# Key factors and bounds of batch 0 shared by all batches, and the value matmuls dealt 5, 5, 4, 4 to the slots

## Chip, cores and metric

One core of one Trainium2 chip runs the whole kernel. The metric is device time in microseconds of one launch; lower is better.

## What is computed

Four batches of 12288 queries attend to 768 pooled keys each; keys and values are the same tensor. The attention's output goes, token by token, through a feed-forward layer of 1024 hidden units with a softmax gate and a normalization.

```python
def _attn_ref(q, kv, w_sr):
    kv_pool = kv.reshape(B, H // r, r, W // r, r, C).mean(axis=(2, 4))   # r = 4
    k = v = kv_pool.reshape(B, -1, C) @ w_sr                             # 768 keys, C = 128
    s = 1 / sqrt(C) * (q @ k.transpose(0, 2, 1))
    a = np.exp(s - s.max(-1, keepdims=True))
    a /= a.sum(-1, keepdims=True) + 1e-09
    return a @ v

def _moe_ref(x, w_in, w_out, g_ln):
    h = x @ w_in                                                         # 128 -> 1024
    e = np.exp(h - h.max(-1))
    solu = h * e / (e.sum(-1) + 1e-09)
    ln = (solu - mean(solu)) / sqrt(var(solu) + 1e-06) * g_ln
    return ln @ w_out                                                    # 1024 -> 128
```

## The kernel before

A tile is 128 tokens; there are 384 tiles, 96 to a batch, and 4 tiles make a group. The order of all work is written out by hand: the loop `for slot in range(NT)` issues, in each of 384 slots, one piece of every stage, each for another tile. Every engine runs its own queue in that order.

In slot S, TensorE (PE) does the scores `s` of tile S+1 (six matmuls of 384 columns, line 518), some of the 18 value matmuls `xa` of a group (512 columns, line 583), the hidden layer `h` of tile S-9 (six of 512 columns, line 636) and the output `o` of tile S-13 (24 of 128 columns, line 764). VectorE (DVE) does the row maximum `nm` of the scores of tile S (line 538), `u` of tile S-11 (line 674), `junkd`, the row maximum of `h`, of tile S-10 (line 644), and the low half of `phl` of tile S (line 549). In the first slot of a group's cycle it also does `xl`, `rz` and `ob`. ScalarE (ACT) does the exponentials `s` and `e`, the high half of `phl`, and `junk`. GpSimd (POOL) splits `u` into a high and a low 16-bit half `uhl` (lines 691 and 698) and adds up the keys of the next batch (`ka`, line 235). SyncE (SP) issues all DMAs of the loop: the transposes `pT` of `phl` and `uT` of `uhl`, and the loads of `q`, of `kv` and the stores of the output.

`s` and `h` share three PSUM buffers. So `s` of tile S+1 waits for `u` of tile S-11 to have read its `h`, and `h` of tile S-9 waits for `phl` of tile S to have read its `s`.

The 18 value matmuls of a group are dealt to four slots by `values` as 4, 5, 5, 4. In each slot but the first, one of them is issued ahead of `s` and the rest behind it. These four slots, called first to fourth below, are those with S mod 4 = 1, 2, 3, 0. A slot that has a matmul of the next batch's keys in it and is a first slot (`with_keys`) deals 3, 5, 5, 5, and its three go behind `o`.

The scores of batch 0 run on 32-bit halves of the keys (`kwh`, `kwl`). Those of batches 1 to 3 run on 16-bit halves `kh`, `kl` of keys scaled by a power of two that follows from the largest key norm of the batch. For each of batches 1 to 3, `key_steps` places the making of the keys at slots 69 to 92 of the batch before: the projection (`kv_k_pe`), squares (`kv_sq`), the norms by a matmul with ones and two maxima on DVE (`kv_norm_pe`, `kv_norm_max`), a scale per channel for the values (`kv_scale_v`), bounds and factors (`kv_bound`, `kv_factors`), `kh` on ACT, `kl` on DVE, and, for batches 1 and 2, the values by matmul with a diagonal (`kv_v_pe`). For batch 3 the values are turned by one DMA transpose (`kv_v_turn`). The loads of the next batch's `kv` and their additions run from slot -30 to slot 65 of a batch, so that one load or another is under way until about slot 253.

After the loop, `in_range` tests that every softmax sum in `z_all` is at least 0.5; where one isn't, the branch `general` computes everything again in a slower way.

Of the kernel before, what the change touches and what calls it, by code (L numbers as in the profile page):

```python
# [58 lines left out]
Z_LEAST = 0.5  # L59

# [4 lines left out]
def kernel(  # L65
# [179 lines left out]
    def kv_k_out(b, half):  # L245
        nc.scalar.copy(half_of("kT", b, half), state.pop(("pk", half))[:, :384])
# [14 lines left out]
    def kv_kh(b, half):  # L261
        nc.scalar.mul(half_of("kh", b, half), half_of("kT", b, half), state["kq", b][:, 0:1])

    def kv_kl(b, half):
        nc.vector.scalar_tensor_tensor(
            half_of("kl", b, half),
            half_of("kT", b, half),
            state["kq", b][:, 0:1],
            half_of("kh", b, half),
            op0=ALU.mult,  # L270
            op1=ALU.subtract,
        )

    def kv_factors(b, half):

        kq = state["kq", b]
        nc.vector.tensor_copy(kq[:, 0:1], state["knm", b][:, 2:3])
        nc.vector.reciprocal(kq[:, 1:2], kq[:, 0:1])
        nc.vector.tensor_scalar(kq[:, 1:2], kq[:, 1:2], SCALE, None, op0=ALU.mult)
# [40 lines left out]
    def kv_bound0(part):  # L320
        knm, bb, sv = state["knm", 0], state["bb", 0], state["sv", 0]
        if part == 0:
            nc.vector.tensor_reduce(knm[:, 2:3], knm[:, 0:2], axis=AX.X, op=ALU.max)
# [29 lines left out]
    def kv_bound(b, part):  # L353
# [13 lines left out]
        elif part == 1:  # L367
# [6 lines left out]
            kv_factors(b, 0)  # L374
# [6 lines left out]
    def kv_diag(b, half):  # L381
        state["dg", b] = bat.tile([P, P], F32, tag="dg", name=f"dg_{b}", bufs=1)
# [35 lines left out]
    def kv_v_scale(b, half):  # L418
# [3 lines left out]
            state["sv", b][:, 0:1],  # L422
# [140 lines left out]
    def values(g, qtr, part):  # L563
        share = {0: [0, 9, 9, 0], 1: [0, 6, 6, 6]}.get(g, [4, 5, 5, 4])
# [6 lines left out]
        cut = s0 + (s0 > 0)  # L571
# [229 lines left out]
    z_all = const.tile([P, NT], F32, name="z_all")  # L801
# [143 lines left out]
    def w_low():  # L945
        nc.gpsimd.tensor_tensor(wcl, gw, wch, op=ALU.subtract)

    fill_front = {1: [partial(kv_norm_max, 0, 0)]}
    fill = {
        0: [partial(kv_norm_pe, 0, 0), partial(kv_scale_v0, 0), w_scale],  # L950
        1: [
            partial(kv_norm_pe, 0, 1), partial(q_split, 1), partial(kv_scale_v0, 1),
            partial(kv_scale_v0, 2), partial(kv_diag, 0, 0), partial(q_low, 1), w_in_low,
        ],
        2: [partial(kv_norm_max, 0, 1), partial(kv_v_pe, 0, 0)],
# [10 lines left out]
        11: [w_low],  # L966
    }
# [44 lines left out]
    FRONT = (kv_scale_v, kv_bound)  # L1012
# [7 lines left out]
    for slot in range(NT):  # L1020
# [53 lines left out]
        for st in pairs:
            for f in st[1:]:
                if f.func is kv_norm_max:
                    f()
# [12 lines left out]
        for st in todo:  # L1090
# [3 lines left out]
            elif len(st) == 1 and st[0].func not in FRONT:  # L1094
# [185 lines left out]
```

## Time and profile before

| | us |
|---|---|
| median of 3 runs | 1868.81 |
| lowest and highest run | 1863.45, 1869.68 |
| the profiled execution's own time | 1865.23 |
| its span, first to last instruction | 1863.4 |
| busy: PE, DVE, ACT, POOL | 1829.8, 1794.2, 1747.4, 1662.0 |

The sums below are made against the profiled execution. A busy share is a mean over stretches; where the loop's steps start, and what an engine waited for just before, is read from the timeline of each engine. All times there are counted from the start of the span. The granted clock of TensorE is 0.999 of full speed over the span.

### The profile page before, as it was taken

What the parts mean: (1) busy time and instruction counts of PE and PEld (TensorE: products, weight loads), DVE (VectorE), ACT (ScalarE), POOL (GpSimd) and SP (SyncE); (2) the same over time, 40 slices, a digit from 0 to 9 for tenths busy, and PEclk for the clock granted to TensorE, in tenths of its full rate; (3) what the DMA queues carried; (4) which work ended last, traced back from release to release, by engine and by line L of the source; (5) the groups of instructions that cost most, each with busy time, mean ns of one, the idle gap of its engine ahead of it and who ended that gap; (6) DMA issues with size and microseconds to landing.
All of it is one profiled execution on the core that took longest, in us unless ns stands there. A gap on an engine that the chain in (4) does not pass through costs nothing.

```text
span 1863.4 us, 42816 instructions
## 1 busy us (share of the span) xinstructions
PE 1829.8 (98%) x15729; PEld 1185.2 (64%) x15729; DVE 1794.2 (96%) x2703; ACT 1747.4 (94%) x3124; POOL 1662.0 (89%) x1466
## 2 busy tenths in 40 slices
PE   8999999999999999999999999999999999999998
PEld 5667777766666656666666666666566666666666
DVE  7999999999999999999999999999999999999997
ACT  5999999999999999999999999999899999999997
POOL 5899999889999999989999999998888888888887
PEclk9999999999999999999999999999999999999999
DMA  8999999999999999999999999999999999999998
GB/s 301 209 225 240 243 240 239 241 225 222 240 232 240 247 227 241 238 239 238 216 242 234 241 240 243 237 237 223 207 227 226 235 228 220 232 227 232 227 216 171
DMA packets 1476891, 432.80 MB, mean 232 GB/s; under 512 B 1404608, under 2 KB 1457984, under 8 KB 1476416
## 3 DMA queue, kind: packets, MB, share of 16 engines
q1 hardware_dynamic: 1476528, 429.97, 113.7%
q8 instruction: 126, 2.06, 0.5%
q14 instruction: 93, 0.76, 0.1%
q10 hardware_dynamic: 144, 0.00, 0.0%
HBM read 52.50 MB, written 25.17 MB: 42 GB/s over the span
## 4 chain that ended last, share of the span: by engine, by line
PE 72%; DVE 9%; POOL 6%; DMA 5%; issue 4%; ACT 3%; SPq 0%; POOLq 0%; DVEq 0%; ACTq 0%
PE o L764 21%; PE h L636 20%; PE s L518 16%; PE xa L583 15%; DMA uT<-uhl 4%; POOL uhl L698 3%; DVE junkd L644 2%; DVE phl L549 2%; DVE nm L538 2%; POOL uhl L691 2%; DVE u L674 1%; DMA kv<-in_kv_dram 1%; ACT e L660 1%; ACT junk L739 1%; ACT phl L541 1%
## 5 line engine op out<-in xcount | busy, mean ns | idle before, releaser
L698 POOL TENSOR_TENSOR uhl<-u,uhl 128x1024 f16<-128x1024 f32 x382 | 814.6, 2133 | 31.6
L764 PEld LDWEIGHTS <-uT 128*128 128x128 f16 x9072 | 536.9, 98 | 96.8 <-DMA uT<-uhl 11.1
L764 PE MATMUL o<-wch,uT 128*128 128x128 f16 x6048 | 568.2, 219 | 4.8 <-DMA uT<-uhl 4.6
L764 PE MATMUL o<-wcl,uT 128*128 128x128 f16 x3024 | 525.9, 219 | 0.0
L674 DVE SCALAR_TENSOR_TENSOR u<-h,rz,e 128x1024 f32<-128x1024 f32 x384 | 491.2, 1279 | 22.2 <-ACT e L660 15.4
L691 POOL TENSOR_SCALAR uhl<-u 128x1024 f16<-128x1024 f32 x379 | 396.7, 1047 | 107.0 <-DVE u L674 99.4
L644 DVE TENSOR_SCALAR_CACHE_REDUCE junkd<-h,rz 128x1024 bf16<-128x1024 f32 x384 | 491.0, 1279 | 1.0 <-PE h L636 0.7
L583 PE MATMUL xa<-pT,vhl 128*128 128x512 f16 x1728 | 478.7, 380 | 0.0
L660 ACT ACTIVATE e<-h,nm,rz 128x1024 f32<-128x1024 f32 x384 | 458.5, 1194 | 3.7 <-DVE junkd L644 3.0
L739 ACT ACTIVATE junk<-u,su 128x1024 bf16<-128x1024 f32 x384 | 437.4, 1139 | 0.1
L539 ACT ACTIVATE s<-s,nm 128x768 f32<-128x768 f32 x384 | 334.5, 871 | 55.0 <-DVE nm L538 53.8
L538 DVE TENSOR_REDUCE nm<-s 128x1 f32<-128x768 f32 x384 | 365.0, 951 | 20.2 <-PE s L518 16.8
L549 DVE SCALAR_TENSOR_TENSOR phl<-s,phl 128x768 f16<-128x768 f32 x384 | 366.0, 953 | 1.7 <-ACT phl L541 1.4
L541 ACT ACTIVATE phl<-s 128x768 f16<-128x768 f32 x384 | 311.5, 811 | 12.1
L636 PEld LDWEIGHTS <-xh 128*128 128x128 f16 x1536 | 138.3, 97 | 214.8 <-issue 35.6
L583 PEld LDWEIGHTS <-vhl 128*128 128x128 f16 x1728 | 162.0, 98 | 132.9 <-issue 12.8
L636 PE MATMUL h<-w_in_h,xh 128*128 128x512 f16 x768 | 228.9, 379 | 9.2 <-DVE rz L618 5.4
L636 PE MATMUL h<-w_in_h,xl 128*128 128x512 f16 x768 | 228.4, 379 | 0.0
L636 PE MATMUL h<-w_in_l,xh 128*128 128x512 f16 x768 | 228.3, 379 | 0.0
L518 PEld LDWEIGHTS <-qh 128*128 128x128 f16 x1152 | 109.2, 98 | 68.3 <-DVE u L674 4.8
L518 PE MATMUL s<-kh,qh 128*128 128x384 f16 x576 | 140.8, 326 | 3.6 <-DVE u L674 3.6
L518 PE MATMUL s<-kh,ql 128*128 128x384 f16 x576 | 140.7, 326 | 0.0
(161 smaller groups left out, 1813.7 us busy)
## 6 DMA issues: line engine op xcount, KB each, us to landing
kv<-in_kv_dram SPq DMA_DIRECT2D x64, 384.0 KB, 4.4
qf<-in_q_dram SPq DMA_DIRECT2D x96, 256.0 KB, 3.3
out_dram<-ob SPq DMA_DIRECT2D x96, 256.0 KB, 2.8
pT<-phl SPq DMA_TRANSPOSE x384, 3.9
uT<-uhl SPq DMA_TRANSPOSE x378, 4.3
raw_in<-in_moe_w_in_dram SPq DMA_DIRECT2D x1, 1024.0 KB, 5.6
raw_out<-in_moe_w_out_dram SPq DMA_DIRECT2D x1, 1024.0 KB, 10.0
room<-uhl SPq DMA_TRANSPOSE x5, 3.9
```

What stands on the lines that cost most here:

```text
L518: nc.tensor.matmul(s[:, half, :384], lh[:, ts], rh[:, half * 384 : (half + 1) * 384], start=n == 0, stop=n == 2,)
L538: nc.vector.tensor_reduce(nm, s, axis=AX.XY, op=ALU.max, negate=True)
L549: nc.vector.scalar_tensor_tensor(phl[:, 1], state.pop(("s", t)), SC, phl[:, 0], op0=ALU.mult, op1=ALU.subtract)
L583: nc.tensor.matmul(xa, v[:, c, :], pT[:, :, a * NKC + c, :], start=n == 0, stop=n == len(seq) - 1)
L636: nc.tensor.matmul(h[:, hs], lh[:, ts], rh[:, hs], start=n == 0, stop=n == 2)
L644: nc.vector.tensor_scalar(junk, state["h", t], state["rz", g][1][:, j : j + 1], None, op0=ALU.mult, op1=ALU.min, accum_out=nm,)
L660: nc.scalar.activation(e, state["h", t], AF.Exp, bias=nm, scale=state["rz", g][0][:, js], accum_out=state["z2", g][:, js],)
L674: nc.vector.scalar_tensor_tensor(u, state.pop(("h", t)), state["rz", g][2][:, j : j + 1], state.pop(("e", t)), op0=ALU.mult, op1=ALU.mult, ...
L691: nc.gpsimd.tensor_scalar(uhl[:, 0, :], u, 1.0, 1.0, op0=ALU.mult, op1=ALU.mult)
L698: low.tensor_tensor(uhl[:, 1, :], u, uhl[:, 0, :], op=ALU.subtract)
L739: nc.scalar.activation(junk, u, AF.Square, scale=-float(DFF), bias=su, accum_out=state["v3", g][:, j : j + 1],)
L764: nc.tensor.matmul(po[:, ts], uT[:, a * NFC + c, :], w[:, c, :], start=start, stop=stop)
```

## The change

Batches 1 to 3 no longer have factors and bounds of their own. `sv` (scales per channel), `bb` (bounds), `kq` (factors), `knm` and the diagonal `dg` are those of batch 0. In batch 0 the largest key norm is replaced by the sum of all squares over 1024, a matmul of two columns (`kv_total_pe`) and one sum of two (`kv_total`); the bounds take a factor 32 for it. The keys of later batches are scaled by batch 0's factor as they leave PSUM (`kv_k_out`), so `kh` is a plain copy and `kl` a subtraction, which moves from DVE to POOL. `kv_norm_pe`, `kv_norm_max`, `kv_scale_v`, `kv_bound` and `kv_diag` are gone from the loop for batches 1 to 3. A step at slot 302 (`kv_fit`) puts six values for each channel into new columns of `z_all`, so that the test at the end also covers whether batch 0's scales fit the channel sums of the others. The values of batches 1 and 2 are made at slot 81 in place of 85. Groups of batches 1 to 3 deal their value matmuls 5, 5, 4, 4, and the second slot has none ahead of `s`.

```diff
-            ("kss", 2, F32, 1),
-            ("knm", 3, F32, 1),
+            ("kss", 2, F32, 4),
             ("vf", NK, F32, 1),
-            ("sv", 2, F32, 2),
-            ("bb", 5, F32, 2),
-            ("kq", 2, F32, 2),
+        for n, w in (("knm", 3), ("sv", 2), ("bb", 5), ("kq", 3), ("dg", P)):
+            state[n, b] = (
+                state[n, 0]
+                if 0 < b < B
...
     def kv_k_out(b, half):
-        nc.scalar.copy(half_of("kT", b, half), state.pop(("pk", half))[:, :384])
+        pk = state.pop(("pk", half))[:, :384]
+        if b < B:
+            nc.scalar.mul(half_of("kT", b, half), pk, state["kq", b][:, 0:1])
...
     def kv_kh(b, half):
-        nc.scalar.mul(half_of("kh", b, half), half_of("kT", b, half), state["kq", b][:, 0:1])
+        nc.scalar.copy(half_of("kh", b, half), half_of("kT", b, half))
 
     def kv_kl(b, half):
-        nc.vector.scalar_tensor_tensor(
...
+        nc.gpsimd.tensor_tensor(
+            half_of("kl", b, half), half_of("kT", b, half), half_of("kh", b, half), op=ALU.subtract
+        )
...
+    def kv_rescale():
+        small(state["dg", 0], state["dg", 0], state["kq", 0][:, 2:3])
+        nc.gpsimd.tensor_tensor(
+            root, state["sv", 0][:, 0:1], state["kq", 0][:, 2:3], op=ALU.mult
+        )
+
+    def kv_fit():
+        low, high = z_all[:, NT : NT + B - 1], z_all[:, NT + B - 1 :]
+        for b in range(1, B):
+            nc.gpsimd.tensor_tensor(
+                fit[:, b - 1 : b], state["kss", b][:, 0:1], state["kss", b][:, 1:2], op=ALU.add
+            )
+        small(fit[:, : B - 1], fit[:, : B - 1], root, 1.0 / SC)
+        small(low, fit[:, : B - 1], root, FIT_LEAST / SC)
+        nc.gpsimd.tensor_scalar(
+            high, low, -1.0 / FIT_LEAST, FIT_MOST, op0=ALU.mult, op1=ALU.add
+        )
...
+    def kv_total_pe():
+        state["pn", 0] = kv_psum(0, "pn_0")
+        nc.tensor.matmul(
+            state["pn", 0][:, :2], onesm, state["kss", 0], start=True, stop=True
+        )
...
     def values(g, qtr, part):
-        share = {0: [0, 9, 9, 0], 1: [0, 6, 6, 6]}.get(g, [4, 5, 5, 4])
+        share = {0: [0, 9, 9, 0], 1: [0, 6, 6, 6]}.get(
+            g, [4, 5, 5, 4] if wide(g + 2) else [5, 5, 4, 4]
+        )
...
-        cut = s0 + (s0 > 0)
+        cut = s0 + (s0 > 0 and (qtr > 1 or wide(g + 2)))
...
             (69, 0, kv_k_pe, kv_k_out), (73, 1, kv_k_pe, kv_k_out),
-            (86, 0, kv_kh), (87, 1, kv_kh),
-            (87, 0, kv_kl), (88, 1, kv_kl),
             (72, 0, kv_sq), (75, 1, kv_sq),
-            (78, 0, kv_scale_v), (79, 1, kv_scale_v), (80, 2, kv_scale_v),
-            (77, 0, kv_norm_pe, kv_norm_max), (81, 1, kv_norm_pe, kv_norm_max),
-            (83, 0, kv_bound), (84, 1, kv_bound), (85, 2, kv_bound),
+            (77, 0, kv_kh), (79, 1, kv_kh),
+            (78, 0, kv_kl), (80, 1, kv_kl),
...
-                (81, 0, kv_diag),
-                (85, 0, kv_v_pe, kv_v_out), (87, 0, kv_v_high), (88, 0, kv_v_low),
+                (81, 0, kv_v_pe, kv_v_out), (83, 0, kv_v_high), (84, 0, kv_v_low),
                 (89, 1, kv_v_pe, kv_v_out), (91, 1, kv_v_high), (92, 1, kv_v_low),
```

Three places show how the order moves. On PE, in the second slot of a group of batch 2 (its values `xa`, the scores `s` of the next tile, `o` of an earlier one), before:

```order
L764 LDWEIGHTS uT_14684
L764 MATMUL o_14819<-wch,uT_14684 128x128
L583 LDWEIGHTS vhl_7656
L583 MATMUL xa_14801<-pT_14429,vhl_7656 128x512
L518 LDWEIGHTS qh_14547
L518 MATMUL s_14861<-kh_7654,qh_14547 128x384
```

and now:

```order
L798 MATMUL o_14748<-wcl,uT_14616 128x128
L798 LDWEIGHTS uT_14616
L798 MATMUL o_14748<-wch,uT_14616 128x128
L550 LDWEIGHTS qh_14480
L550 MATMUL s_14789<-kh_7617,qh_14480 128x384
```

The value matmul that stood between `o` and `s` is gone from there; five follow `s` in place of four, and the third slot has three behind `s` in place of four.

On DVE, at slots 179 to 181 (slots 83 to 85 of batch 1, where the bounds `bb` and factors of batch 2 were made between the four steps of each tile), before:

```order
L549 SCALAR_TENSOR_TENSOR phl_12774<-s_12694,phl_12774 128x768
L360 TENSOR_REDUCE knm_7649<-knm_7649 128x1
L361 TENSOR_SCALAR bb_7652<-knm_7649,wmax_99 128x1
L364 TENSOR_SCALAR knm_7649<-knm_7649 128x1
L538 TENSOR_REDUCE nm_12842<-s_12780 128x1
L674 SCALAR_TENSOR_TENSOR u_12847,su_12848<-h_12724,rz_12702,e_12796 128x1024
L644 TENSOR_SCALAR junkd_12869,nm_169_12868<-h_12804,rz_12702 128x1024
L549 SCALAR_TENSOR_TENSOR phl_12845<-s_12780,phl_12845 128x768
L368 TENSOR_SCALAR bb_7652<-bb_7652 128x1
```

and now:

```order
L581 SCALAR_TENSOR_TENSOR phl_12731<-s_12651,phl_12731 128x768
L570 TENSOR_REDUCE nm_12794<-s_12736 128x1
L708 SCALAR_TENSOR_TENSOR u_12799,su_12800<-h_12683,rz_12659,e_12752 128x1024
L678 TENSOR_SCALAR junkd_12821,nm_169_12820<-h_12761,rz_12659 128x1024
L581 SCALAR_TENSOR_TENSOR phl_12797<-s_12736,phl_12797 128x768
L570 TENSOR_REDUCE nm_12868<-s_12803 128x1
```

Nothing but the tiles' own steps is left; over the whole program DVE has 80 instructions fewer.

On POOL, at slots 173 to 175 (slots 77 to 79 of batch 1), before:

```order
L235 TENSOR_TENSOR ka_12312<-kv_0_11505,kv_1_12088 128x384
L95 TENSOR_SCALAR sv_7651<-sv_7651 128x1
L96 TENSOR_TENSOR sv_7651<-sv_7651,mhalf 128x1
L691 TENSOR_SCALAR uhl_12489<-u_12478 128x1024
L698 TENSOR_TENSOR uhl_12489<-u_12478,uhl_12489 128x1024
L505 TENSOR_TENSOR ql_12468<-qf_12015,qh_12467 128x512
L691 TENSOR_SCALAR uhl_12560<-u_12546 128x1024
```

and now:

```order
L240 TENSOR_TENSOR ka_12275<-kv_0_11468,kv_1_12051 128x384
L725 TENSOR_SCALAR uhl_12448<-u_12438 128x1024
L732 TENSOR_TENSOR uhl_12448<-u_12438,uhl_12448 128x1024
L537 TENSOR_TENSOR ql_12431<-qf_11978,qh_12430 128x512
L274 TENSOR_TENSOR kl_7618<-kT_7613,kh_7617 128x384
L725 TENSOR_SCALAR uhl_12519<-u_12505 128x1024
```

The scale's steps are gone and the first half of `kl` stands behind `ql`, ahead of the next tile's `uhl`. SP's queue holds the same DMAs in the same order; the one transpose of batch 3's values was there already.

## Rows read from the trace of the kernel before

**Rows 1.** The page, part 1: busy time, share of the span, instructions.

```profile
PE 1829.8 (98%) x15729; PEld 1185.2 (64%) x15729; DVE 1794.2 (96%) x2703; ACT 1747.4 (94%) x3124; POOL 1662.0 (89%) x1466
```

**Rows 2.** Timeline, DVE, slots 317 to 321: start, us, instruction [idle before <-releaser].

```profile
1507.55 0.96 DVE L538 TENSOR_REDUCE nm<-s 128x1 f32<-128x768 f32 x1
...
1513.95 1.27 DVE L674 SCALAR_TENSOR_TENSOR u<-h,rz,e 128x1024 f32<-128x1024 f32 x1
...
1522.67 1.28 DVE L674 SCALAR_TENSOR_TENSOR u<-h,rz,e 128x1024 f32<-128x1024 f32 x1 [0.18 <-ACT e L660]
...
1525.09 0.95 DVE L549 SCALAR_TENSOR_TENSOR phl<-s,phl 128x768 f16<-128x768 f32 x1
1526.09 0.96 DVE L538 TENSOR_REDUCE nm<-s 128x1 f32<-128x768 f32 x1
```

**Rows 3.** Timeline, PE, the same group, its first and second slot.

```profile
1512.04 0.59 PE L583 MATMUL xa<-pT,vhl 128*128 128x512 f16 x2
1512.59 0.59 PE L636 MATMUL h<-w_in_h,xh 128*128 128x512 f16 x2
...
1515.22 0.38 PE L583 MATMUL xa<-pT,vhl 128*128 128x512 f16 x1
1515.44 0.49 PE L518 MATMUL s<-kh,qh 128*128 128x384 f16 x2
```

**Rows 4.** Timeline, DVE: nm at slots 65, 69, 93, 165, 169, 181, 185, 189, 257, 261, 285, 381.

```profile
310.12 0.96 DVE L538 TENSOR_REDUCE nm<-s 128x1 f32<-128x768 f32 x1 [0.24 <-PE s L518]
328.85 0.96 DVE L538 TENSOR_REDUCE nm<-s 128x1 f32<-128x768 f32 x1 [0.24 <-PE s L518]
448.74 0.96 DVE L538 TENSOR_REDUCE nm<-s 128x1 f32<-128x768 f32 x1 [0.44 <-PE s L518]
784.92 0.96 DVE L538 TENSOR_REDUCE nm<-s 128x1 f32<-128x768 f32 x1
804.23 0.96 DVE L538 TENSOR_REDUCE nm<-s 128x1 f32<-128x768 f32 x1 [0.37 <-PE s L518]
863.11 0.95 DVE L538 TENSOR_REDUCE nm<-s 128x1 f32<-128x768 f32 x1
885.07 0.94 DVE L538 TENSOR_REDUCE nm<-s 128x1 f32<-128x768 f32 x1
904.14 0.96 DVE L538 TENSOR_REDUCE nm<-s 128x1 f32<-128x768 f32 x1 [0.37 <-PE s L518]
1221.78 0.96 DVE L538 TENSOR_REDUCE nm<-s 128x1 f32<-128x768 f32 x1
1240.32 0.96 DVE L538 TENSOR_REDUCE nm<-s 128x1 f32<-128x768 f32 x1
1359.23 0.96 DVE L538 TENSOR_REDUCE nm<-s 128x1 f32<-128x768 f32 x1
1804.20 0.96 DVE L538 TENSOR_REDUCE nm<-s 128x1 f32<-128x768 f32 x1
```

**Rows 5.** Groups by line and form: count | busy us, mean ns | idle before.

```profile
L265 DVE SCALAR_TENSOR_TENSOR kl<-kT,kq,kh 128x384 f16<-128x384 f32 x6 | 12.3, 2051 | 0.0
L411 POOL TENSOR_TENSOR vhl<-vf,vhl 128x384 f16<-128x384 f32 x6 | 5.8, 969 | 0.0
L299 DVE TENSOR_REDUCE knm<-pn 128x1 f32<-128x384 f32 x8 | 4.4, 547 | 0.0
```

**Rows 6.** Timeline, SP's queue of DMAs: in batch 1, then in batch 3.

```profile
652.52 3.80 SPq L713 DMA_TRANSPOSE uT<-uhl  x1
656.38 0.57 SPq L471 DMA_DIRECT2D qf<-in_q_dram  x1
...
1518.84 1.85 SPq L713 DMA_TRANSPOSE uT<-uhl  x1
1521.65 1.41 SPq L552 DMA_TRANSPOSE pT<-phl  x1
```

**Rows 7.** Waits: engine line waited for: us in total, times, longest us.

```profile
PEld L764 <- DMA uT<-uhl: 11.1, 14, 1.6
```

More of the change, by code (lines that the diff above doesn't have):

```diff
@@ L59 @@
 Z_LEAST = 0.5
+FIT_LEAST = 32.0
+FIT_MOST = 4.4
+FIT_AT = 302
 SOON = {0: (), 1: (11, 12), 2: (21, 27), 3: (33, 39), 4: (45, 47), 5: (51, 54)}
@@ L245, in kv_k_out @@
     def kv_k_out(b, half):
-        nc.scalar.copy(half_of("kT", b, half), state.pop(("pk", half))[:, :384])
+        pk = state.pop(("pk", half))[:, :384]
+        if b < B:
+            nc.scalar.mul(half_of("kT", b, half), pk, state["kq", b][:, 0:1])
+        else:
+            nc.scalar.copy(half_of("kT", b, half), pk)
     def kv_wide_h(b, half):
@@ L261, in kv_kh, with kv_factors @@
     def kv_kh(b, half):
-        nc.scalar.mul(half_of("kh", b, half), half_of("kT", b, half), state["kq", b][:, 0:1])
+        nc.scalar.copy(half_of("kh", b, half), half_of("kT", b, half))
     def kv_kl(b, half):
-        nc.vector.scalar_tensor_tensor(
[L266 to L271, printed above, removed]
-        )
[L274 to L279, printed above, removed]
+        nc.gpsimd.tensor_tensor(
+            half_of("kl", b, half), half_of("kT", b, half), half_of("kh", b, half), op=ALU.subtract
+        )
+    def kv_factors():
+        kq = state["kq", 0]
+        nc.vector.tensor_copy(kq[:, 0:1], state["knm", 0][:, 2:3])
+        nc.vector.reciprocal(kq[:, 2:3], kq[:, 0:1])
+        nc.vector.tensor_scalar(kq[:, 1:2], kq[:, 2:3], SCALE, None, op0=ALU.mult)
+    def kv_rescale():
[14 more added lines that the diff above has]
+        )
     def kv_sq(b, half):
@@ L286, in kv_sq, with kv_total @@
             accum_out=state["kss", b][:, half : half + 1],
+        )
[4 more added lines that the diff above has]
+        )
+    def kv_total():
+        nc.vector.tensor_reduce(
+            state["knm", 0][:, 2:3], state.pop(("pn", 0))[:, :2], axis=AX.X, op=ALU.add
         )
@@ L332, in kv_bound0 @@
         else:
-            small(bb[:, 1:2], bb[:, 0:1], SC * 1e-3 * 2.0**15)
-            small(bb[:, 0:1], bb[:, 0:1], SC)
+            small(bb[:, 1:2], bb[:, 0:1], SC / 32 * 1e-3 * 2.0**15)
+            small(bb[:, 0:1], bb[:, 0:1], SC / 32)
             small(bb[:, 2:3], bb[:, 1:2], 1e-9)
@@ L381, in kv_diag @@
     def kv_diag(b, half):
-        state["dg", b] = bat.tile([P, P], F32, tag="dg", name=f"dg_{b}", bufs=1)
         nc.gpsimd.tensor_scalar(
@@ L421, in kv_v_scale @@
             half_of("kT", b, half),
-            state["sv", b][:, 0:1],
+            root,
             1.0,
@@ L563, in values @@
     def values(g, qtr, part):
[L564 removed]
+        share = {0: [0, 9, 9, 0], 1: [0, 6, 6, 6]}.get(
+            g, [4, 5, 5, 4] if wide(g + 2) else [5, 5, 4, 4]
+        )
         if with_keys(g):
@@ L798, in final_out @@
         nc.sync.dma_start(rows.rearrange("(j p) c -> p j c", p=P), ob)
-    z_all = const.tile([P, NT], F32, name="z_all")
+    z_all = const.tile([P, NT + 2 * (B - 1)], F32, name="z_all")
+    fit = const.tile([P, B], F32, name="fit")
+    root = fit[:, B - 1 : B]
     ident = const.tile([P, P], F32, name="ident")
@@ L966 @@
         11: [w_low],
+        14: [kv_factors],
+        17: [kv_rescale],
+        FIT_AT: [kv_fit],
     }
@@ L1027 @@
         todo = plan.pop(slot, [])
-        for st in todo:
-            if len(st) == 1 and st[0].func in FRONT:
-                st[0]()
         at(slot, scores_exp)
-        for f in fill_front.get(slot, []):
-            f()
         if slot <= LH:
@@ L1069 @@
             for f in st[1:]:
-                if f.func is not kv_norm_max:
-                    f()
+                f()
         if slot >= LH:
             at(slot, scores_split)
[L1074 to L1077, printed above, removed]
         at_soon(slot - NORM, values_recip)
@@ L1093 @@
                     f()
-            elif len(st) == 1 and st[0].func not in FRONT:
+            elif len(st) == 1:
                 st[0]()
@@ L1106, in in_range @@
             state["inside"] = const.tile([P, 1], BF16, name="inside")
-            good = const.tile([P, NT], BF16, name="good")
+            good = const.tile([P, NT + 2 * (B - 1)], BF16, name="good")
             nc.vector.tensor_scalar(
```

11 lines of the change are left out of this document (4 added, 7 removed).

## The prediction

> **What bounds the kernel now.** I read the busy shares first [rows 1]: PE 98%, DVE 96%, ACT 94%. With engines so even, no share says what a change is worth, so the next view is the timeline of DVE, taken at one row that every tile has, `nm`, at the first slot of groups. Its starts cut the span into stretches [rows 4]. From slot 285 to 381 (batch 3, 24 groups) it takes 444.97 us, 18.54 a group. From slot 65 to 69 (batch 0, 32-bit scores) it takes 18.73. From slot 189 to 257 (batch 2 with loads of `kv` in flight, 17 groups) 317.64, 18.69 a group. And the six groups of slots 69 to 93 of batches 0, 1 and 2, in which the next batch's keys are made, take 119.89, 119.22 and 118.91 us, where 112.38 (six of 18.73), 111.24 and 111.24 would be the plain loop: 7.51, 7.98 and 7.67 too much, 23.2 us together. That is where the change works first.
>
> What holds the plain loop at 18.54 is seen on DVE and PE in one group. On DVE [rows 2] one `nm` of a first slot starts at 1507.55 and the next at 1526.09. Just before the latter `phl` began at 1525.09 and took 0.95. DVE instructions follow each other with an overlap of about 0.08, so `nm` could have started at 1525.96; it waited 0.13 for its scores. Before that `u` waited for `e` of ACT. Take the 0.13 away, and a chain of DVE and ACT alone is left: 18.41 a group. On PE [rows 3] value matmuls start 0.22 apart (1515.22, then 1515.44). The two of 1512.04 are through at 1512.48, but `h` starts at 1512.59, since `phl` has to read its buffer first: PE idles 0.11 in the first slot.
>
> **The keys leave DVE (forecast -16.3).** Per transition DVE loses two `kl` of 2.05 us, two maxima of 0.55 [rows 5], 5.2 us, and twenty-odd steps of one column. All of it stood between the steps of tiles on an engine that has next to no idle time, so it goes from the time as it stands. What stays is what PE does for the keys: projections at slots 69 and 73, values at 81 and 89 (batches 1 and 2 only). A group with such matmuls took 19.31 (slots 165 to 169) and 19.07 (slots 185 to 189, without any work on DVE for the keys) [rows 4]: 0.77 and 0.53 over 18.54. I take 0.6 for each; there are 4 + 4 + 2 = 10 of them, 6.0 us.
>
> ACT keeps its number of instructions; the scale moves from `kh` to `kT`. `kh` now stands at slots 77 and 79, the first hidden because ACT waits for `nm` in the second slot, the second in front of an `e` that DVE waits for. POOL gets two `kl`; its subtraction of the same shape takes 0.97 [rows 5]. POOL loses two steps for the scale, two for the bounds and the diagonal at the same slots, so its sum stays about level, but the values' split moves up to slots 83 and 84, in groups which are now 2 to 3.5 us shorter. `uhl` may come late, and behind it SP's transposes and `o`. I put 0.3 a transition for ACT and POOL together, 0.9; bounds 0 and 3. Sum: 23.2 - 6.0 - 0.9 = 16.3; bounds 23.2 - 5.3 = 17.9 and 23.2 - 7.7 - 3.0 = 12.5.
>
> One rule speaks against this part. `kl` on DVE takes 2.05 us, the norms' maximum over as many columns, out of PSUM, 0.55 [rows 5]: `kl` has both tensors in SBUF and seems to stand behind a POOL instruction. The Trainium skill, Perfetto Trace Analysis, section Optimizing Scalar/DVE Operations, says that GpSimd and DVE share an SBUF read port, so that moving work between the two might not help. By it the six `kl` would come back on DVE as waits, up to 5.8 us (six of 0.97), and the sum would be -10.5. The rows beside it speak against that: the four steps DVE does in these slots read at least one operand from PSUM, and none of them is longer next to the long POOL subtractions. So I leave it out.
>
> **The deal 5, 5, 4, 4 (forecast -5.6).** In the first slot a fifth value matmul fills the 0.11 for which PE waited, so `h` comes 0.11 later there. In the second slot nothing stands ahead of `s`, which gets 0.22 back: it starts 0.11 earlier, at 1515.33. It may not start before `u` of that slot is through, which starts on DVE at 1513.95 and takes 1.27 [rows 2], so it is through at 1515.22 and `s` hardly waits. `h` of the second slot then starts as now, behind `phl`. From there to the scores for which `nm` waited at 1526.09, PE has one value matmul less: they come 0.22 earlier. DVE waited 0.13 for them, so 0.13 is the gain, and the chain of DVE and ACT sets the end. Lower bound 0 (another wait takes its place).
>
> The groups that start at slots 97 to 377 have the new deal, 71, less six that deal 3, 5, 5, 5: 65. For the 29 from slot 257 on: 29 x 0.13 = 3.8 us. For the other 36, with loads of `kv` in flight, I do not trust it. There SP's queue issues without a break (`uT` at 652.52 for 3.80 us, the next DMA at 656.38), where in batch 3 it waits for its data (done at 1520.69, next at 1521.65) [rows 6], and PE waited 11.1 us in 14 places for `uT` [rows 7]. These groups took 18.69 though their own chain needs 18.54; a shorter chain finds the queue no faster. I take 0.05 each, 1.8 us; bounds 0 and 36 x 0.13 = 4.7.
>
> **The front and the rest (forecast -0.3).** In slots 1 and 2 two maxima of 0.55 become one sum of two columns; three steps of one column come to DVE at slot 14. Bounds 0 and -1. `kv_fit` is six small POOL steps once, where POOL waits for `u` anyway: 0, at most 1.5. SP's order is the same. The wider test at the end is a few columns.
>
> **The sum.** 16.3 + 3.8 + 1.8 + 0.3 = 22.2 us. The profiled execution's own time is 1865.23; 1865.23 - 22.2 = 1843.0. The three runs of before go from 1863.45 to 1869.68 with the median at 1868.81, 3.6 above the profiled one. I keep 1843 and let the range take that up.
>
> **Rivals.**
>
> *The DMA queue keeps it (1850).* The long transitions gave the queue time to catch up. Without them it runs behind from slot 69 to 257, 47 groups that took 892.9. If it needs 18.9 a group, a little more than the 18.69 seen, they take 888.3: 4.6 saved in place of 4.8 + 5.3 + 1.8 (transitions of batches 0 and 1, 7.51 and 7.98 less 4 x 0.6 and 0.3 each, and the deal), so 7.3 less. For it: SP without a break. Against: 18.69 was seen with the queue full.
>
> *All of it pays (1835).* The queue has room, and the 11.1 us of waits for `uT` thin out. -17.9 - 3.8 - 4.7 - 1.0 = -27.4, and some 3 us of the waits: 1835. The Trainium skill, DMA: Bandwidth & Descriptors, section Latency and other measured facts, has DMA transposes at 261 GB/s where the middle dimension is not contiguous; a group transposes 3.67 MB (`pT` and `uT` of four tiles), an estimate by that figure of 14.1 us out of 18.5, which leaves room for the loads and would put the sum at 1840. SP's unbroken issues say otherwise.
>
> *The deal backfires (1863).* With nothing ahead of `s` in the second slot, `s` waits there for `u`. If the wait eats the whole moved matmul and `h` slips with it, 65 groups lose up to 0.22 in place of gaining: 14.3 lost, 5.6 not gained, 1843 + 19.9 = 1863. Against: `u` is through 0.1 us before PE gets there.
>
> *Slower: the branch is taken (over 3600).* `general` runs if one of the six new values in any channel is under 0.5. It does all four batches again, at least another span. It decides if a later batch's channel sum is under 1/64 or over 4 times what batch 0's scale allows. The scale is a power of two within a factor 4 of batch 0's sum, and all batches are drawn alike with 768 keys to a sum, so the sums agree within some tenths. It needs an error in the test itself.
>
> **Chances and range.** Forecast 0.62, queue 0.16, all pays 0.14, backfires 0.06, branch 0.02. The bounds of the forecast's terms give 1865.23 - 12.5 - 0 - 0 + 1.5, about 1854, to 1835; the range is 1835 to 1853. About 0.3%, 5.6 us, is what a measurement can tell from no change. Faster by more than that: 0.95; within it (the dear half of backfiring): 0.03; slower: 0.02.
>
> **What would show it.** `nm` to `nm` over slots 69 to 93: 115, 114 and 113 us, with 19.1 in groups with key matmuls and about 18.6 in the others; over slots 285 to 381, 18.41 a group; `nm` without a wait for `s` in the first slots, `h` without one in the first slot. SP without a break from slot 69 to 257. It is wrong if the loop of batch 3 stays at 18.54 (the deal does nothing), if DVE shows long steps beside `kl` on POOL, or if waits of PE for `uT` grow beyond 20 us.

## The result, and the profile after

The changed kernel takes 1848.97 us (median of 6 runs, 1848.35 to 1851.94), the kernel before 1869.24 (6 runs, 1863.45 to 1871.91): a ratio of 0.9895, 95% interval 0.9884 to 0.9906, 20.3 us less. Forecast were 22.2 less, 1843.0, in a range of 1835 to 1853. The two profiled executions are only 13.3 us apart, 1865.23 and 1851.94: that of before lies 4.0 under its median, that of after 3.0 over its own. So a stretch of one profile is held against the other only where it repeats from run to run, and the medians settle the rest.

The page of after, part 1 (answers to [rows 1]). The engines are as even as before, and DVE carries out 68 instructions fewer (2703, now 2635):

```profile
PE 1819.7 (98%) x15723; PEld 1188.4 (64%) x15723; DVE 1771.3 (96%) x2635; ACT 1741.2 (94%) x3124; POOL 1661.0 (90%) x1466
```

The timeline of DVE after, `nm` at slots 69, 93, 165, 189, 261, 285 and 381 (answers to [rows 4]; start, us, instruction, idle before):

```profile
330.31 0.96 DVE L570 TENSOR_REDUCE nm<-s 128x1 f32<-128x768 f32 x1 [0.24 <-PE s L550]
445.58 0.96 DVE L570 TENSOR_REDUCE nm<-s 128x1 f32<-128x768 f32 x1 [0.44 <-PE s L550]
783.93 0.96 DVE L570 TENSOR_REDUCE nm<-s 128x1 f32<-128x768 f32 x1 [0.50 <-PE s L550]
899.32 0.96 DVE L570 TENSOR_REDUCE nm<-s 128x1 f32<-128x768 f32 x1 [0.37 <-PE s L550]
1236.52 0.96 DVE L570 TENSOR_REDUCE nm<-s 128x1 f32<-128x768 f32 x1 [0.22 <-PE s L550]
1349.46 0.95 DVE L570 TENSOR_REDUCE nm<-s 128x1 f32<-128x768 f32 x1
1790.81 0.94 DVE L570 TENSOR_REDUCE nm<-s 128x1 f32<-128x768 f32 x1
```

The differences of these starts, beside those of before and the forecast:

| slots | before | after | forecast |
|---|---|---|---|
| 69 to 93, keys of batch 1 | 119.89 | 115.27 | 115 |
| 165 to 189, keys of batch 2 | 119.22 | 115.39 | 114 |
| 261 to 285, keys of batch 3 | 118.91 | 112.94 | 113 |
| 93 to 165, loads in flight | 336.18 | 338.35 | no longer |
| 189 to 261, loads in flight | 336.18 | 337.20 | no longer |
| 285 to 381, no loads | 444.97 | 441.35 | 441.8 |

The transitions came out within 1.4 us of the forecast, the plain loop within 0.5. What did not come out is the groups with loads of `kv` in flight: in this pair of profiles they got longer by 2.2 and 1.0 us, and `nm` at slot 69, behind other groups with loads, starts 1.5 us later (330.31, before 328.85).

The mechanism of the deal, in the same group of batch 3 as [rows 2, 3]. DVE first, then PE:

```profile
1496.58 0.95 DVE L570 TENSOR_REDUCE nm<-s 128x1 f32<-128x768 f32 x1
...
1502.96 1.28 DVE L708 SCALAR_TENSOR_TENSOR u<-h,rz,e 128x1024 f32<-128x1024 f32 x1
...
1514.97 0.95 DVE L570 TENSOR_REDUCE nm<-s 128x1 f32<-128x768 f32 x1
```

```profile
1500.56 1.24 PE L617 MATMUL xa<-pT,vhl 128*128 128x512 f16 x5
1501.63 0.59 PE L670 MATMUL h<-w_in_h,xh 128*128 128x512 f16 x2
...
1504.30 0.48 PE L550 MATMUL s<-kh,qh 128*128 128x384 f16 x2
```

Five value matmuls, 0.22 apart, now run up to `h`: the 0.11 for which PE idled is filled. In the second slot `s` starts at 1504.30, right behind `u`, which is through at 1504.24. The last `nm` stands right at the end of the `phl` before it and waits for nothing; from `nm` to `nm` it is 18.39.

The waits of after over the whole span (in total us, times, longest). PE's weight loads wait 27.1 us for `uT`, where before they waited 11.1 [rows 7]:

```profile
PEld L798 <- DMA uT<-uhl: 27.1, 32, 1.9
DVE nm L570 <- PE s L550: 25.4, 64, 1.6
```

### The profile page after: what moved, and what is told of

The parts are those of the page before. It is cut to its first block, busy times and chain, and to the rows that moved or that the text cites. A ratio compares the mean times of both kernels' runs of the same rounds, so it can differ in the third digit from the quotient of the medians.

```text
span 1850.2 us, 42743 instructions
## 1 busy us (share of the span) xinstructions
PE 1819.7 (98%) x15723; PEld 1188.4 (64%) x15723; DVE 1771.3 (96%) x2635; ACT 1741.2 (94%) x3124; POOL 1661.0 (90%) x1466
## 4 chain that ended last, share of the span: by engine, by line
PE 43%; DVE 14%; ACT 14%; POOL 13%; issue 9%; DMA 7%; SPq 0%; DVEq 0%; POOLq 0%
PE o L798 13%; PE h L670 11%; PE s L550 10%; PE xa L617 8%; POOL uhl L732 6%; DMA uT<-uhl 5%; ACT e L694 4%; ACT junk L773 4%; DVE junkd L678 4%; DVE nm L570 4%; ACT phl L573 3%; POOL uhl L725 3%; DVE phl L581 3%; ACT s L571 1%; DVE u L708 1%
## 5 line engine op out<-in xcount | busy, mean ns | idle before, releaser
L798 PEld LDWEIGHTS <-uT 128*128 128x128 f16 x9072 | 535.9, 98 | 109.0 <-DMA uT<-uhl 27.1
L617 PE MATMUL xa<-pT,vhl 128*128 128x512 f16 x1728 | 468.9, 380 | 0.6 <-DMA pT<-phl 0.5
```

The source lines that it names most:

```text
L617: nc.tensor.matmul(xa, v[:, c, :], pT[:, :, a * NKC + c, :], start=n == 0, stop=n == len(seq) - 1)
L798: nc.tensor.matmul(po[:, ts], uT[:, a * NFC + c, :], w[:, c, :], start=start, stop=stop)
```

## The experiments

The changed kernel's median in these comparisons is 1848.97; it did not run again beside them. The kernel before did, with medians of 1867.3 to 1870.2, and the ratios below are to those.

**1. What the deal is worth, and where.** First the changed kernel with the old deal, then the old kernel with the new one.

```diff
-            g, [4, 5, 5, 4] if wide(g + 2) else [5, 5, 4, 4]
+            g, [4, 5, 5, 4]
...
-        cut = s0 + (s0 > 0 and (qtr > 1 or wide(g + 2)))
+        cut = s0 + (s0 > 0)
```

> The changed kernel with the value matmuls dealt 4, 5, 5, 4 again in all batches, all else as changed. The changed kernel took 1848.97. Queue theory: from slot 33 to 257, where loads of kv are in flight, SP's queue sets the pace (18.7 to 18.8 us a group, SP idle for 0.03 to 0.04 a group), so the deal is worth something only in the 29 groups from slot 257 on, 18.54 against 18.39: 29 x 0.15 = 4.3, time 1853. Chain theory (the deal pays in all 65 groups that have it, the loads do not matter): 65 x 0.15 = 9.8, time 1859. Prediction on record: 5.6, time 1854.5. In the trace: slots 285 to 381 at 18.54 a group by all of them.

Measured: 1852.95 (1849.16 to 1859.24), ratio to before 0.9917, interval 0.9897 to 0.9937; 4.0 us over the changed kernel.

The other way round, the same two lines of the new kernel put into the kernel before:

> The kernel before with nothing but the new deal 5, 5, 4, 4 in batches 1 to 3. The kernel before took 1869.24. Queue theory: -4.3, 1865, nothing of it in slots 97 to 257. Chain theory: -9.8, 1859. If the deal helps only together with the shorter transitions, 1869. In the trace: slots 285 to 381 at 18.39 a group by the first two, 18.54 by the last.

Measured: 1864.9 against 1868.22 beside it, ratio 0.9973, interval 0.996 to 0.9985: 3.3 us by the medians, 5.0 by the ratio. The intervals are wide, so the places are needed too. `nm` at slots 97, 165, 285 and 381 of the kernel before with the new deal:

```profile
467.97 0.96 DVE L538 TENSOR_REDUCE nm<-s 128x1 f32<-128x768 f32 x1 [0.24 <-PE s L518]
786.96 0.94 DVE L538 TENSOR_REDUCE nm<-s 128x1 f32<-128x768 f32 x1
1363.03 0.95 DVE L538 TENSOR_REDUCE nm<-s 128x1 f32<-128x768 f32 x1
1804.30 0.95 DVE L538 TENSOR_REDUCE nm<-s 128x1 f32<-128x768 f32 x1
```

Slots 285 to 381 take 441.27, 18.39 a group as in the changed kernel (and 444.94 in the run with the old deal). Slots 97 to 165 take 318.99, where before took 317.40: nothing is gained there, though the trace has many groups of 18.39 among them; others of 19 to 21 give it back. In the changed kernel the same slots take 319.50 with the new deal and 320.38 with the old, so single profiles do not tell a few hundredths a group there. Both medians are far from the chain theory's 1859, and the queue theory stands: 24 groups of 0.15, 3.6 us, and nothing that can be told from the loaded ones. The transition ahead of them, slots 261 to 285, takes 113.03 with the old deal and 112.94 with the new, so the groups in it add about 0.1, not their 0.15 each.

**2. What the loaded groups wait for.** Every second load of the later batches is left out, in the changed kernel and in the kernel before.

```diff
     def kv_load(b, pos):
 
+        if pos % 2:
+            state["kv", b, pos] = state["kv", b, pos - 1]
+            return
```

> The changed kernel with every second load of kv for batches 1 to 3 left out (24 of 48; the additions on POOL stay and add the tile of the load before once more, so keys of batches 1 to 3 are wrong). It asks what makes the groups of slots 9 to 261 longer than the plain loop: in the changed kernel's profile they are 3.0, 6.9 and 6.1 us over it in three stretches outside the transitions. Queue theory: with half the loads SP's queue has room, the 16 us go, time 1834, 18.39 a group from slot 97 to 165, SP idle over 0.5 us a group. Rival (POOL's additions delay uhl, the queue only follows): nothing changes, 1848 to 1849.

> The kernel before with the same half of the loads left out. Queue theory: before had only 5.5 us of excess in its profiled execution, and some 4 more in its median run, so it goes from 1869 to 1860, and the change is then worth 1860 - 1834 = 26 us in place of 20: the queue had kept 6 of it. Rival (the queue keeps nothing of the change; loads cost both kernels the same): the difference stays at 20.

Measured: 1837.69 (1837.41 to 1838.04) and 1861.19 (1860.54 to 1861.70). Not 1834, but 11.3 us came off the changed kernel and 7.0 off the one beside 1868.22. The change is worth 23.5 us with half the loads (26 were expected), 20.3 with all of them. The scatter goes too: runs of before spread over 8.5 us with all loads, over 1.2 with half. `nm` at slots 69, 93, 97, 165, 189, 261 and 285, of the changed kernel with half the loads, then of before with half:

```profile
327.34 0.96 DVE L573 TENSOR_REDUCE nm<-s 128x1 f32<-128x768 f32 x1 [0.24 <-PE s L553]
442.61 0.96 DVE L573 TENSOR_REDUCE nm<-s 128x1 f32<-128x768 f32 x1 [0.44 <-PE s L553]
461.46 0.96 DVE L573 TENSOR_REDUCE nm<-s 128x1 f32<-128x768 f32 x1 [0.24 <-PE s L553]
774.06 0.95 DVE L573 TENSOR_REDUCE nm<-s 128x1 f32<-128x768 f32 x1
888.31 0.96 DVE L573 TENSOR_REDUCE nm<-s 128x1 f32<-128x768 f32 x1 [0.37 <-PE s L553]
1219.73 0.94 DVE L573 TENSOR_REDUCE nm<-s 128x1 f32<-128x768 f32 x1
1332.64 0.95 DVE L573 TENSOR_REDUCE nm<-s 128x1 f32<-128x768 f32 x1
```

```profile
327.94 0.96 DVE L541 TENSOR_REDUCE nm<-s 128x1 f32<-128x768 f32 x1 [0.24 <-PE s L521]
447.84 0.96 DVE L541 TENSOR_REDUCE nm<-s 128x1 f32<-128x768 f32 x1 [0.44 <-PE s L521]
466.62 0.96 DVE L541 TENSOR_REDUCE nm<-s 128x1 f32<-128x768 f32 x1 [0.30 <-PE s L521]
781.77 0.96 DVE L541 TENSOR_REDUCE nm<-s 128x1 f32<-128x768 f32 x1
900.76 0.96 DVE L541 TENSOR_REDUCE nm<-s 128x1 f32<-128x768 f32 x1 [0.37 <-PE s L521]
1234.46 0.96 DVE L541 TENSOR_REDUCE nm<-s 128x1 f32<-128x768 f32 x1
1353.36 0.96 DVE L541 TENSOR_REDUCE nm<-s 128x1 f32<-128x768 f32 x1
```

From slot 97 to 165 it is 312.60 and 315.15 for 17 groups: 18.39 and 18.54, the plain loop of each. With fewer loads the deal pays there too. POOL's additions were still there, so they are not the cause. In this pair, undisturbed by loads, the transitions (slots 69 to 93, 165 to 189, 261 to 285) give 4.63, 4.74 and 5.99 us, 15.4 together. One sign did not come: gaps of over 0.2 us in SP's queue were to add up to over 0.5 us a group in slots 97 to 161, and come to 0.14 (0.04 in the changed kernel), though no group waits. So an unbroken queue of SP by itself is no sign of a bound.

The same from the other side, 16 more loads in batch 3 that nothing reads:

```diff
             plan.setdefault((b - 1) * TPB + k, []).append(fs)
+    for pos in range(RR):
+        plan.setdefault((3 * TPB + 6 * pos) // GT * GT, []).append([partial(kv_load, 3, pos)])
```

> The changed kernel with 16 more loads of kv (384 KB each) in batch 3, where it has none, at the spacing of the other batches; nothing reads them and POOL adds nothing. Queue theory: bytes alone fill the queue, the groups of batch 3 go from 18.39 to the 18.7 to 18.8 of the others, 23 groups x 0.36 = 8, time 1857, and SP's wait falls from 1.1 us a group to under 0.1. Rival (batch 3 has room for them, 18.39 stays): 1849.

Measured: 1857.63, 8.7 us more than the changed kernel; slots 285 to 381 take 448.54, 18.69 a group. Loads alone do it, without POOL's additions. How many bytes the DMA engines move is seen in the busy times of a stretch (last three columns: granted clock, DMA share, GB/s; behind PE its busy us): before at slots 97 to 161; after there and, in its second row, in batch 3; half the loads at slots 97 to 161; the extra loads in batch 3:

```profile
467.52:766.38 298.86, 297.12 (x2593) 186.36 (x2592) 291.59 (x433) 286.35 (x513) 278.81 (x245) 1.00 1.19 239
```

```profile
464.43:764.96 300.53, 295.23 (x2594) 187.26 (x2593) 291.12 (x433) 286.00 (x513) 278.68 (x245) 1.00 1.19 238
1400.00:1800.00 400.00, 399.98 (x3525) 254.92 (x3523) 394.26 (x589) 386.44 (x696) 351.99 (x311) 1.00 1.16 228
```

```profile
461.46:755.67 294.21, 294.21 (x2594) 187.64 (x2593) 289.99 (x432) 284.70 (x513) 278.55 (x245) 1.00 1.19 237
```

```profile
1366.62:1796.78 430.16, 424.35 (x3727) 268.73 (x3726) 418.37 (x623) 411.00 (x737) 373.58 (x329) 1.00 1.20 238
```

With all loads, PE idles 5.3 of 300.5 us after the change and 1.7 of 298.9 before; with half it idles for nothing. What PE waits for there is `uT`. Its weight loads' waits in slots 97 to 161 before and after, then in batch 3 with the extra loads (in slots 97 to 161 with half the loads, and in batch 3 of the changed kernel, there is none):

```profile
PEld L764 <- DMA uT<-uhl: 3.9, 5, 1.6
```

```profile
PEld L798 <- DMA uT<-uhl: 10.1, 14, 1.6
```

```profile
PEld L798 <- DMA uT<-uhl: 14.8, 22, 1.8
```

So loads in flight make `uT` late, and that is what the loaded groups wait for. That a ceiling on bytes is behind it is inferred and not shown. For it: none of these long stretches passes 239 GB/s, and at 238 GB/s a group of after moves 238 x 18.78 = 4.47 MB, which in 18.39 us would be 243. Against it: the stretch with half the loads runs at 237 and waits for nothing, and over a shorter stretch the kernel before moved 247:

```profile
605.62:652.20 46.58, 46.43 (x406) 28.96 (x404) 45.35 (x67) 44.91 (x81) 43.42 (x38) 1.00 1.19 247
```

**3. Whether the loads can be made cheaper.** Two attempts: each load split into two of 192 KB, and the loads issued by POOL. The first (its `kv_load` then fetches one half):

```diff
...
-            yield slot // GT * GT, [partial(kv_load, b, pos)]
+            for half in range(2):
+                yield slot // GT * GT + 2 * half, [partial(kv_load, b, pos, half)]
```

> The changed kernel with each load of kv (384 KB) split into two of 192 KB, two slots apart; same bytes. Half the loads less had given 11.3. Theory (the DMA queue as a whole is full in slots 33 to 257, SP idle under 0.1 us a group): splitting moves nothing, 1847 to 1851. Rival (it is the burst of 384 KB ahead of a uT that stalls PE): most of the 11 comes back, 1838 to 1841, and the groups over 19 us vanish from slots 97 to 165.

Measured: 1850.55 (1848.14 to 1853.04), ratio 0.9906, interval 0.9888 to 0.9925: no gain. Four of the 17 groups of slots 97 to 165 still take over 19 us, where the changed kernel has five. Twice as many loads in SP's queue with the same bytes cost nothing that can be told, so it is the bytes that count and not the number of issues. Then the loads issued by POOL:

```diff
-        nc.sync.dma_start(
+        (nc.sync if b == 1 and pos in SOON else nc.gpsimd).dma_start(
```

> The changed kernel with the loads of kv in the loop issued by POOL in place of SP; same bytes. Theory (the 16 DMA engines behind the queue are full, whoever issues): no gain, 1849, or up to 10 more if POOL pays for each of the 42 issues. Rival (SP's own queue, which holds the transposes behind a load, is the bound): up to 11 less, 1838.

Measured: 1874.19 (1868.61 to 1887.44), 25 us more, well over the 10 that were allowed for. The 42 issues cost POOL 0.63 us each, 26.4 together:

```profile
L229 POOL DMA_DIRECT2D kv<-in_kv_dram x42 | 26.4, 629 | 0.1
```

The rate in slots 97 to 161 was 233 GB/s, not higher, and over the span PE's weight loads waited longer for `uT`, 38.7 us in 46 places against 27.1 in 32. So the burst is not the limit, and nothing speaks for SP's queue as the limit; but POOL's own 26.4 us come into this run, so the issuer is not cleanly separated. The Trainium skill, DMA: Bandwidth & Descriptors, section SWDGE vs HWDGE vs iDMA, says that DMAs issued from SP and from GpSimd run on the same SDMA engines; the 233 GB/s are in keeping with it, and no run here shows it by itself.

**4. What `kl` costs, and where it may go.** On DVE again, at the new slots, in the changed kernel:

```diff
     def kv_kl(b, half):
-        nc.gpsimd.tensor_tensor(
+        nc.vector.tensor_tensor(
```

> The changed kernel (1848.97) with kl, the low half of the keys, made on DVE again, by a plain subtraction at the new places (slots 78 and 80), where both its operands lie in SBUF. If DVE waits there for POOL, as in the kernel before, each of the six takes about 2.05 us and all of it shows: 6 x 2.05 = 12.3, time 1861. Rival (2.05 belonged to the old places at slots 87 and 88 or to the product in it): 0.55 each, 3.3, time 1852.

Measured: 1857.72, 8.75 us more: between the two, nearer the first. From its own trace, by form, then the same from the trace of after:

```profile
L274 DVE TENSOR_TENSOR kl<-kT,kh 128x384 f16<-128x384 f32 x6 | 10.6, 1772 | 0.0
```

```profile
L274 POOL TENSOR_TENSOR kl<-kT,kh 128x384 f16<-128x384 f32 x6 | 5.5, 917 | 0.0
```

The groups of slots 77 to 81 take 21.79, 21.78 and 22.01 in place of 18.93, 18.65 and 18.65: 9.4 us more for 10.6 of `kl`. Nearly all of DVE's time is the kernel's time.

Why `kl` takes so long on DVE is seen where it stood in the kernel before. Two of its six, each with the subtraction of `uhl` that was running on POOL:

```profile
1332.41 2.13 POOL L698 TENSOR_TENSOR uhl<-u,uhl 128x1024 f16<-128x1024 f32 x1
1332.50 2.46 DVE L265 SCALAR_TENSOR_TENSOR kl<-kT,kq,kh 128x384 f16<-128x384 f32 x1
...
1338.24 2.13 POOL L698 TENSOR_TENSOR uhl<-u,uhl 128x1024 f16<-128x1024 f32 x1
1339.02 1.76 DVE L265 SCALAR_TENSOR_TENSOR kl<-kT,kq,kh 128x384 f16<-128x384 f32 x1
```

`kl` started 0.09 and 0.78 us after the subtraction, took 2.46 and 1.76, and ended 0.42 and 0.41 after its end. So did all six there and all six of this run: whenever it started, `kl` ended 0.41 to 0.42 us after POOL's instruction. It waited for POOL, whether it held a product (as in the kernel before) or not, at the old places and at the new.

Next, `kl` on DVE out of PSUM, straight behind the projection:

```diff
...
+            state.pop(("pk", half))[:, :384],
+            state["kq", b][:, 0:1],
...
-            (69, 0, kv_k_pe, kv_k_out), (73, 1, kv_k_pe, kv_k_out),
+            (69, 0, kv_k_pe, kv_k_out, kv_kh, kv_kl), (73, 1, kv_k_pe, kv_k_out, kv_kh, kv_kl),
```

> The changed kernel with kl on DVE, but made from the projection while that is still in PSUM (slots 69 and 73, with kh right behind it on ACT): same engine, same columns, one operand in PSUM. If it is the second operand in SBUF that lets DVE stand, kl takes 0.55 to 0.6 here, 6 x 0.6 = 3.6, time 1852 to 1853, and in the trace no kl is over 0.7. Rival (kl is long on DVE wherever POOL is at work, whatever it reads): 2.05 each, 1861.

Measured: 1876.97, 28 us more. The instruction took as long as the theory had it, the kernel did not:

```profile
L274 DVE SCALAR_TENSOR_TENSOR kl<-pk,kq,kh 128x384 f16<-128x384 f32 x6 | 3.7, 618 | 17.4 <-ACT kh L271 17.4
```

That is 0.62 each, but DVE stood 17.4 us in front of it, since `kh` on ACT comes late in the same slot. That wait was not costed. Nor does the 0.62 settle the question: by the time that `kh` was there, POOL had finished its `uhl` and ran nothing beside any of the six `kl`, so the rival is not put to the test. What speaks for the operand in PSUM is `phl`, which reads one operand from there: in the 26 places of after where it ran wholly inside such a subtraction of POOL it took 0.95 us, as elsewhere. Then the move of `kl` to POOL by itself, in the kernel before, at its old slots 87 and 88:

```diff
-        nc.vector.scalar_tensor_tensor(
...
+        scaled = state["ksq", b].bitcast(F32)
+        nc.gpsimd.tensor_scalar(
+            scaled, half_of("kT", b, half), state["kq", b][:, 0:1], 1.0, op0=ALU.mult, op1=ALU.mult
+        )
+        nc.gpsimd.tensor_tensor(
+            half_of("kl", b, half), scaled, half_of("kh", b, half), op=ALU.subtract
+        )
```

> The kernel before (1868) with kl alone moved from DVE to POOL, as a product and a subtraction there, at the same slots; maxima, bounds and factors stay on DVE for each batch. If DVE's time is what the transitions cost, the group that holds kl (slots 85 to 89: 22.1, 22.0, 22.4 us) loses what putting kl back cost in the changed kernel (8.75 us for six), time 1859, and the groups at slots 77 to 85 keep their 19.3 and 20.5. If POOL's work (9 us more in these slots) delays uhl, less comes back: 1862 to 1868. If the whole transition term comes from kl: 1853.

Measured: 1866.71 against 1868.6, ratio 0.9993, interval 0.998 to 1.0006: not told from no change. `nm` at slots 85, 89 and 93, and DVE's `rz` between the last two:

```profile
407.93 0.95 DVE L537 TENSOR_REDUCE nm<-s 128x1 f32<-128x768 f32 x1
427.25 0.96 DVE L537 TENSOR_REDUCE nm<-s 128x1 f32<-128x768 f32 x1 [0.44 <-PE s L517]
434.14 0.20 DVE L617 RECIPROCAL rz<-zz 128x8 f32<-128x8 f32 x1 [2.00 <-POOL zz L609]
448.39 0.96 DVE L537 TENSOR_REDUCE nm<-s 128x1 f32<-128x768 f32 x1 [0.45 <-PE s L517]
```

The group that held `kl` falls from 22.10 to 19.32; the next rises from 19.31 to 21.14, since POOL now has the product, `kl` and a half of `vhl` ahead of `zz`, for which DVE waits 2.0. The other two transitions read the same (2.9 and 3.2 off, 2.5 and 2.2 on). So in the kernel before, moving `kl` alone gains little: the three groups lose 8.9 us together and the next ones take back 6.5. Last, the changed kernel with `kh` and `kl` at the old slots:

```diff
-            (77, 0, kv_kh), (79, 1, kv_kh),
-            (78, 0, kv_kl), (80, 1, kv_kl),
+            (86, 0, kv_kh), (87, 1, kv_kh),
+            (87, 0, kv_kl), (88, 1, kv_kl),
```

> The changed kernel with kh and kl at the old places again (kh at slots 86 and 87, kl on POOL at 87 and 88). In the kernel before, kl moved to POOL at these places saved 2.8 to 3.2 us in its group and lost 1.8 to 2.5 in the next, where DVE's rz waited 2.0 us for POOL's zz: ahead of zz stood the product 0.57, kl 0.92 and a half of vhl 0.91. If it is the place itself (kl ahead of zz) that costs, 1.8 to 2.5 in each of three transitions, time 1854.5 to 1856.5, with rz waiting for zz. If it was the pile at that place (product and vhl, which the changed kernel does not have there), rz waits under 0.3 us and the time is 1849 to 1850.

Measured: 1856.0 (1851.45 to 1861.10), ratio 0.9922, interval 0.9898 to 0.9946, which overlaps that of the changed kernel (0.9884 to 0.9906). The waits of `rz`:

```profile
DVE rz L652 <- POOL zz L644: 0.8, 3, 0.5
```

That is 0.8 us in 3 places, hardly more than the changed kernel's 0.7 in 2, with the same longest of 0.5 (under 0.3 was expected): the pile, not the place, held `rz` up. The median is 7 us over the changed kernel's, as by the other theory, but `rz` hardly waits, and the intervals overlap. In the trace batch 0's transition is unchanged, those of batches 1 and 2 are 1.0 and 0.9 us longer, and most of the rest lies in groups with loads. Whether the late place costs anything is left open; if it does, it isn't by `zz`.

**5. The deal in batch 0.**

```diff
-            g, [4, 5, 5, 4] if wide(g + 2) else [5, 5, 4, 4]
+            g, [5, 5, 4, 4]
...
-        cut = s0 + (s0 > 0 and (qtr > 1 or wide(g + 2)))
+        cut = s0 + (qtr > 1)
```

> The changed kernel with the deal 5, 5, 4, 4 in batch 0 too. In batch 0 a group takes 18.73 us and nm waits 0.24 us for its scores, but PE shows no gap over 0.06 us there (the 32-bit scores take it longer). If PE has no room, the order of its work changes nothing: 1849, slots 57 to 69 at 18.73 a group. Rival (as in batch 3, the wait of nm goes): 0.13 to 0.24 for some 20 groups, 2.6 to 4.8 less, 1844 to 1846.

Measured: 1849.94 (1845.95 to 1854.03), ratio 0.9896, interval 0.988 to 0.9913: no change. Slots 57 to 65 took 18.81 a group, 0.08 more than with the old deal. The gain that the rival forecast did not come.

None of these runs that does all the loads beats the changed kernel.

## Why the prediction was right, point by point

**The keys leave DVE: right.** Forecast were 16.3 us less; the undisturbed pair shows 15.4 (4.63, 4.74, 5.99 against 4.8, 5.3, 6.2), and the medians less the deal's 3.7 and the front's 0.7 leave 15.9. The reason given, that DVE's time goes from the time as it stands, is borne out for `kl` by putting it back: 8.75 of 10.6 us show. The rest, the maxima and the steps of one column, was not put back by itself. The 0.6 for a group with the keys' matmuls holds: in the changed kernel with half the loads the ten take 6.0 together over 18.73 and 18.54, though the 19.31 that it was read from held 0.2 us of loads (with half of them the kernel before takes 19.09 there). The term that was too small is the 0.9 for ACT and POOL. What is left over the plain loop in those three transitions is 7.6 us (2.89, 3.01 and 1.67), 1.5 more than the 6.0. What the forecast got by luck is the place: it did not ask whether slots 87 and 88 would have done for `kl` on POOL. In the kernel before, most of the gain was given back there.

**The rule on moving work from DVE to GpSimd: rightly left out, by half a reason.** I held against it that DVE's other steps read PSUM. That held: with `kl` on POOL `phl` takes at most 0.96 us and `u` at most 1.29, as before. What the prediction left at "seems" is shown by the traces: on DVE `kl` did stand behind POOL. But work on POOL came back another way when it stood ahead of `zz`, and this I had not weighed.

**The deal in batch 3: right.** 0.13 a group was forecast for 29 groups, 3.8 us. 0.15 came in the 24 from slot 285 on, 3.6, and about 0.1 in the transition ahead of them: 3.7. The wait of `nm`, the gap ahead of `h` and the start of `s` behind `u` all read as forecast in the group shown. Backfiring did not happen.

**The deal with loads in flight: 1.8 us that no run shows.** The step is "I take 0.05 each". Undoing the deal costs 4.0 us and making it alone gains 3.3 to 5.0; less the 3.7 without loads, 0.3 and -0.4 to 1.3 are left for 36 groups, within the scatter of the runs. So 0 fits better than 1.8, which is not excluded. That the loads keep the gain is shown: with half of them the same groups have it, 0.15 each. The reason for my distrust was the right one (a shorter chain finds the queue no faster); carried through, it gives 0, and the rival "the DMA queue keeps it" was its consistent form. That rival was too dear at 7.3, because it assumed 18.9 a group; the runs show about 3 kept, 23.5 less 20.3. It is luck that the measured 1848.97 lies by its 1850: set against the median of before, 1869.24, the rival comes to 1854.3 and the forecast to 1847.0, and the forecast is the nearer.

**The front: a little too small.** `nm` at slot 9 starts 0.69 us earlier (48.70 in place of 49.39), and the other traces have it at 48.4 to 48.8 with the new front and at 49.2 to 49.5 with the old, the run with POOL's issues, 49.1, left aside; 0.3 was forecast.

**The sum.** 15.4 + 3.7 + 0 + 0.7 = 19.8 against the 20.3 measured, which by its interval is 17.6 to 21.7. That it comes so near is in part luck, since 15.4 was read with half the loads; in the profiles with all of them the transitions give 14.4 (4.62, 3.83 and 5.97). The forecast was taken from the profiled 1865.23, 4.0 below the median of before; of the 6.0 us by which 1848.97 lies over 1843.0, this baseline explains 4.0 and the sum the other 2.

**What was to show it wrong.** Waits of PE for `uT` over 20 us were named as such a sign, and the profiled execution, 3.0 us over its median, has 27.1. By this sign the prediction was wrong about the groups with loads, though not about the time: what `uT` held up there is the part of the gain that was kept.

**All of it pays: excluded.** 1848.97 is 14 us over its 1835, and the waits for `uT` grew in place of thinning out. The estimate by 261 GB/s for DMA transposes (the Trainium skill, DMA: Bandwidth & Descriptors, section Latency and other measured facts) left room for the loads. No run here has the transposes by themselves, so the figure is not tested; with loads beside them the DMA engines moved at most 239 GB/s over a long stretch, and the room was not there.

## What to carry to other kernels

When the engines are even, find the stretches with different limits first, and cost an edit in each by that stretch's own limit: the same edit was worth 0.15 us a group where DVE and ACT set the pace and nothing that could be told where loads made `uT` late. Whether transfers hold a stretch is not read from their rate (237 GB/s without a wait, 238 with waits) or from an unbroken queue, but from the waits for them and from a run with fewer of them. Where they hold it, a gain of the engines is taken to be zero, not "a little". And work moved to another engine is costed by what stands behind it in that engine's queue at the very place, not by that engine's sum.

## What the runs showed of the hardware

A step on DVE of 128 x 384 with both operands in SBUF (`kl`) that started while POOL's `uhl` subtraction ran ended 0.41 to 0.42 us after that, whether it had started 0.09 or 0.78 us into it, so that it took 1.76 to 2.46 us. The like step with one operand in PSUM took 0.62 while POOL ran nothing, and the subtraction on POOL 0.92. The Trainium skill, SBUF — State Buffer, section Who interferes with whom, says that a DVE instruction with two SBUF inputs contends with a GpSimd instruction that reads SBUF, over a shared port that one of them holds locked; the twelve `kl` on DVE that end 0.41 to 0.42 us behind POOL agree with it.

The scatter of this kernel's runs comes with the loads: with all of them the runs of the changed kernel spread over 3.6 us and those of before over 8.5, with half the loads over 0.6 and 1.2.
